# Feed-forward block size by backlog, order of left-over tiles, and a fourth part in the weight conversion

## The chip, the cores and the metric

The kernel runs on one core of a Trainium2 chip. The metric is the device time of one execution in microseconds (us). The engines named below are PE (TensorE, the matmuls), DVE (VectorE), ACT (ScalarE), POOL (GpSimd) and SP (SyncE, which issues the DMAs). Each has its own queue and works through it in order.

## The reference

Attention in which each query keeps only its 32 largest scores, then a feed-forward layer with a hard-swish gate. Eight batches, eight heads, 576 tokens, head size 64; the feed-forward layer sees 4608 tokens of width 512 and has 2048 hidden units. The two weight matrices come as 64-bit floats.

```python
def _attn_ref(q, k, v):
    scores = scale * np.matmul(q, k.transpose(0, 1, 3, 2))
    kth = np.partition(scores, -top_k, axis=-1)[..., -top_k:-top_k + 1]   # top_k = 32
    scores = np.where(scores >= kth, scores, -1000000000.0)
    scores = scores - np.max(scores, axis=-1, keepdims=True)
    attn = np.exp(scores)
    attn = attn / (np.sum(attn, axis=-1, keepdims=True) + 1e-09)
    return np.matmul(attn, v)

def _moe_ref(x, w_in, w_out):
    h = x @ w_in
    g = h * np.clip(h + 3.0, 0.0, 6.0) / 6.0
    return g @ w_out
```

## The kernel before

**Duos.** The 576 queries of a head are four tiles of 128 (query `t` of the loop takes every fourth row) and 64 left-over rows. A *pair* is two heads; a *duo* (class `Duo`, L184) is one query tile of two pairs, so four heads. A batch has ten duos: eight full ones (two halves times four tiles) and two left-over ones (`rest`), whose 64 rows of two heads are stacked to 128 partitions, so they have half as much DVE work. In all there are 80 duos; the list `duos` (L401 to L411) fixes their order. Before the change a left-over duo stands after tile 0 and after tile 2, so at places 2 and 7 of a batch; in the last batch both stand at places 2 and 3.

**Parts of a duo.** `scores` (L199): PE multiplies queries and keys into the PSUM tile `big`, ACT copies them to `sc`. `top` (L242): DVE finds the 32 largest in four rounds of MAX8 (L249) and three of MATCH_REPLACE8 (L253). `shift` (L258, POOL), `exp` (L267, ACT: L272 and L277, and the sum `den`, L282), `inverse` (L284, DVE: the reciprocal, L286), `weights` (L288, POOL: two multiplications at L296 and a copy to `e16` that splits words into 16-bit halves, L305), `flip` (L308: a DMA transpose, issued by SP), `join` (L313: a copy back to `eT`, L317, on ACT for the first half of a duo, u=0, and on POOL for the second, u=1), and `values` (L325: 40 matmul records `pv`, L337, and an ACT copy to `xT` or `xr`, L344).

**Order.** Nothing is scheduled automatically: each engine executes in the order in which the program's main loop (L548 to L578) emits. The loop runs over duos `m`, and within each over eight slots `i`. A slot emits one top round of duo `m` (slots 0 to 3 for u=0, 4 to 7 for u=1), one step of weight conversion, in slot 1 the scores of duo `m+1`, and then the parts that fall due (`parts`, L541). The tables at L524 to L535 say in which slot, counted from a duo's first, each part falls due: `usual` has the reciprocal of u=0 in slot 7 and `values` in slot 20, so in slot 4 of duo `m+2`. There, `values` of duo `m-2` is emitted right ahead of `exp` of duo `m`. Slot 5 also transposes the keys and queries of a pair of the next batch in four duos of each batch.

**Feed-forward.** Once `values` has filled a block of tokens, `queue` (L437) puts a generator `feed_forward` (L348) on `todo`. It is worked off in *pieces* (L420): a piece is eight matmuls of `h` (L361) for 128 tokens, or four for 256, or two of `acc` (L383). A block of 128 tokens has 16 pieces, one of 256 has 32. After each two h pieces come ACT's relu and copy (L369, L371) and POOL's gate (L375, L376), and at the end ACT's scaling to `o` (L393) and the store. `left` counts the pieces queued and not yet emitted. By it each duo takes 6, 7, 8 or 9 pieces (3, 4, 4 or 5 in a left-over duo), spread over its slots:

```python
        level = (left >= 8) + (left >= 16) + (left >= 48)
        count = ((3, 4, 4, 5) if u and u.rest else (6, 7, 8, 9))[level]
```

Blocks have 128 tokens in the first and last batch and 256 in the others (`two`, L465). Left-over rows of two batches make a block of 128 in `xr`. The pool for `xT` has two buffers; so before `values` takes a new one (L467 to L470), it emits all pieces that the block before the last one still has, however many:

```python
            while len(blocks) > 1 and blocks[-2] in todo:
                piece()
```

These are called forced pieces below.

**Weights.** `convert` (L96) turns a chunk of 128 x 512 64-bit floats into 32-bit ones with integer operations. There are 32 chunks, one for each slot from the start. Its parts: the load; then ACT's L108 and L111 and POOL's L109; then DVE's L117 and L118 and POOL's add, L122, which needs L118. `convert_step` (L490) runs one part of the oldest chunk and the first part of a new one.

Of the kernel before, what the change touches and what calls it, by code (L numbers as in the profile page):

```python
# [29 lines left out]
def kernel(  # L30
# [9 lines left out]
    nc = tc.nc  # L40
    P = nc.NUM_PARTITIONS
    B, H, S, D = q.shape
    DM, FF = moe_w_in.shape
    J = S // P
# [51 lines left out]
    def convert(dst, src):  # L96

        st = kqpool.tile([P, 2 * WC], U32, tag="kq", name="st")
        nc.sync.dma_start(st[:], src)
        yield
        words = st[:].rearrange("p (n two) -> p n two", two=2)
        lo, hi = words[:, :, 0], words[:, :, 1]
        a = gpool.tile([P, WC], F32, tag="g", name="a")
        y = gpool.tile([P, WC], F32, tag="g", name="y")
        nc.scalar.activation(a[:], hi.bitcast(F32), AF.Abs)  # L108
        nc.gpsimd.tensor_scalar(a[:], a[:], HI_MOST, HI_LEAST, ALU.min, ALU.max)  # L109

        nc.scalar.activation(y[:], lo, AF.Copy, bias=2.0, scale=2.0**-51)  # L111
        yield

        au, yu = a[:].bitcast(U32), y[:].bitcast(U32)
        nc.vector.tensor_scalar(au, au, 3, None, ALU.logical_shift_left)  # L117
        nc.vector.scalar_tensor_tensor(  # L118
            out=yu, in0=hi, scalar=0x80000000, in1=yu,
            op0=ALU.bitwise_and, op1=ALU.bitwise_or,  # L120
        )
        nc.gpsimd.tensor_tensor(  # L122
            dst.bitcast(I32), a[:].bitcast(I32), y[:].bitcast(I32), ALU.add
        )
# [13 lines left out]
    class Pair:  # L138


        def __init__(self, b, hp):
            self.b, self.hp = b, hp
            self.vm, self.vr, self.kr = vms[hp], vrs[hp], krs[b % 2 * NHP + hp]
# [40 lines left out]
    class Duo:  # L184
# [4 lines left out]


        def __init__(self, pairs, qt):
            self.pairs, self.qt = pairs, qt
            self.rest = qt == J
            self.nt = 1 if self.rest else 2
            self.nb = J + 2 if self.rest else 2 * J + 1
            self.m, self.less = [None] * 2, [None] * 2
            self.e16, self.t16, self.eT = [None] * 2, [None] * 2, [None] * 2
# [115 lines left out]
        def join(self, u):  # L313

            eT = self.eT[u] = kqpool.tile([P, 2 * J + 1, P], F32, tag="kq", name="eT")
            copy = nc.gpsimd.tensor_copy if u else nc.scalar.copy
            copy(  # L317
                eT[:, 0 : self.nb, :]
                .rearrange("p c q -> p (c q)")
                .bitcast(U16)  # L320
                .rearrange("p (x h) -> p h x", h=2),
                self.t16[u][:, 0 : 2 * self.nb, :].rearrange("p (h c) q -> p h (c q)", h=2),
            )
# [77 lines left out]
    pairs = [[Pair(b, hp) for hp in range(NHP)] for b in range(B)]  # L401
    duos = []
    for b in range(B):
        halves = [pairs[b][0:2], pairs[b][2:4]]
        for qt in range(J):
            duos += [Duo(h, qt) for h in halves]

            if b == B - 1 and qt == 0:
                duos += [Duo(h, J) for h in halves]
            elif b < B - 1 and qt % 2 == 0:  # L410
                duos.append(Duo(halves[qt // 2], J))  # L411
    assert J == NHP == 4
    per_batch = 2 * J + 2
    ND = len(duos)
    todo = []
    blocks = []
    left = 0
    gates = []

    def piece(count=1):  # L420
        nonlocal left
        for _ in range(count):
            while todo:
                try:
                    gates.append(next(todo[0]))
                    left -= 1
                    break
                except StopIteration:
                    todo.pop(0)
            else:  # L430
                gates.append(None)
            if len(gates) > 2:
                gate = gates.pop(0)
                if gate:
                    gate()

    def queue(*block):  # L437
        nonlocal left
        todo.append(feed_forward(*block))
        if block[0] is not state.get("xr"):  # L440
            blocks.append(todo[-1])
        left += block[1] // 8

    state = {}

    def values(m):

        u = duos[m]
        b, qt, hp = u.pairs[0].b, u.qt, u.pairs[0].hp
        if u.rest:  # L450
            if b % 2 == 0 and hp == 0:
                state["xr"] = xrpool.tile([P, NHP, P], F32, tag="xr", name="xr")
            u.values(state["xr"][:, hp : hp + 2, (b % 2) * R : (b % 2 + 1) * R])
            if b % 2 == 1 and hp == 2:

                def rows(t0):
                    return [
                        (i * R, (i + 1) * R, out[(b - 1 + i) * S + JP : (b + i) * S, :])
                        for i in range(2)
                    ]  # L460

                queue(state["xr"], P, rows)
            return

        two = 0 < b < B - 1  # L465
        c0 = qt % 2 * P if two else 0
        if hp == 0 and c0 == 0:  # L467
            while len(blocks) > 1 and blocks[-2] in todo:
                piece()
            state["xT"] = xtpool.tile([P, NHP, 2 * P], F32, tag="xT", name="xT")  # L470
        u.values(state["xT"][:, hp : hp + 2, c0 : c0 + P])
        if hp == 2 and (not two or c0):

            def rows(t0):
                t = qt - c0 // P + t0 // P
                return [(0, P, out[b * S + t : b * S + JP : J, :])]

            queue(state["xT"], c0 + P, rows)

    chunks = list(weight_chunks())  # L480
    landing, converting = [], []

    def land(count=1):

        for _ in range(min(count, len(chunks))):
            c = convert(*chunks.pop(0))
            next(c)
            landing.append(c)

    def convert_step(depth=2):  # L490

        if len(converting) >= depth or not landing:
            for c in converting[:1]:
                next(c, None)
            del converting[:1]
        if landing:
            c = landing.pop(0)
            next(c)
            converting.append(c)
        land()  # L500

    def pair_at(m, first):
# [22 lines left out]
        shift0=3, exp0=4, inverse0=7, weights0=8, flip0=10, join0=13,  # L525
        shift1=7, exp1=8, inverse1=11, weights1=12, flip1=14, join1=17, values=20,
    )
    early = dict(
        shift0=3, exp0=3, inverse0=4, weights0=4, flip0=6, join0=8,
        shift1=7, exp1=7, inverse1=8, weights1=8, flip1=10, join1=12, values=13,  # L530
    )
    soon = dict(
        shift0=3, exp0=3, inverse0=5, weights0=5, flip0=7, join0=10,
        shift1=7, exp1=7, inverse1=9, weights1=9, flip1=11, join1=14, values=16,
    )  # L535
    queued = {}
    for m in range(ND):
        for part, at in (early if m < 2 else soon if m >= ND - 2 else usual).items():
            queued.setdefault(8 * m + at, []).append((m, part))

    def parts(slot):  # L541
        for m, part in sorted(queued.get(slot, []), key=lambda x: x[1][:-1] != "shift"):
            if part == "values":
                values(m)
            else:
                getattr(duos[m], part[:-1])(int(part[-1]))

    for m in range(ND + 3):  # L548
        u = duos[m] if m < ND else None

        level = (left >= 8) + (left >= 16) + (left >= 48)
        count = ((3, 4, 4, 5) if u and u.rest else (6, 7, 8, 9))[level]
        for i in range(8):
            if u:
                u.top(i // 4, i % 4)
            convert_step()
            if m == 0 and i == 0:
                first[3].load()
            if m == 0 and i in (1, 2):
                first[i + 1].transpose()  # L560
            if i == (3 if m == 0 else 1) and m + 1 < ND:
                duos[m + 1].scores()
            parts(8 * m + i)
            if m == 0 and i in (1, 4):
                for p in duos[i // 4].pairs:
                    p.load_values()
            if i == 0:
                p = pair_at(m, 4)
                if p:
                    p.load()  # L570
            if i == 3 and u and u.pairs[0].b and 1 <= m % per_batch <= 2:
                for p in duos[m - 1].pairs:
                    p.load_values()
            if i == 5:
                p = pair_at(m, 5)
                if p:
                    p.transpose()
            piece((i + 1) * count // 8 - i * count // 8)  # L578
# [36 lines left out]
```

## Time and profile before

| what | value |
|---|---|
| median of 4 executions | 1632.12 us |
| lowest and highest | 1631.29 and 1633.61 us |
| the profiled execution | 1633.61 us |
| its span on the core | 1631.8 us |
| ACT busy / POOL busy | 1088.5 / 1143.5 us |
| granted PE clock, mean | 0.962 |

The span runs from the first to the last instruction; 1.8 us of the execution's time lie around it. Busy times are sums of an engine's instructions. Lines of the profile have the form: line of the kernel, engine, operation, output, inputs, count. In a timeline a line begins with the start in us from the span's start and the duration; in brackets at its end stands how long the engine was idle ahead of it, and which instruction ended that idle time. A table by stage begins each line with the stretch and its length, then gives busy time and, in brackets, the number of instructions of PE, PEld (weight loads), DVE, ACT and POOL, then the granted clock (1.00 is full), the share of time in which the DMA engines were busy, and GB/s. A line of the waits names the waiting engine and line, the one waited for, and the total, the count and the longest. Below, "duo 27" is the duo with `m` = 27, and PE's lag is how far its queue is behind DVE's.

### The profile page before, as it was taken

To read this page: it belongs to the slowest core of one execution; us is meant where nothing else is said; L and a number is where in the kernel's file an instruction comes from. 1 tells how busy PE (TensorE), PEld (TensorE's weight loads), DVE (VectorE), ACT (ScalarE), POOL (GpSimd) and SP (SyncE) were. 2 spreads that over 40 slices of the span, in tenths; PEclk is the share of its full clock that TensorE was granted. 3 is DMA by queue.
4 is the path that set the end of the run, shared out by engine and by line. 5 is a ranking of instruction groups with operands and counts; after the bars stand their busy time and mean duration, and the time that the engine had idled before them with its cause. 6 is when DMAs were issued, how large, how long until landed. Compare 5 with 4: busy or idle time off the path is not lost.

```text
span 1631.8 us, 25648 instructions
## 1 busy us (share of the span) xinstructions
PE 1471.1 (90%) x8736; PEld 982.6 (60%) x8736; DVE 1470.2 (90%) x3105; ACT 1088.5 (67%) x1863; POOL 1143.5 (70%) x1266
## 2 busy tenths in 40 slices
PE   5237699849999999898999999898999999899999
PEld 3134567527567584756567584656567584657775
DVE  5999999999999989999999889999999889999500
ACT  5566677757777676767767676767767676757521
POOL 3887577757687775867777776867787776867741
PEclk9968799979999999999999999999999999999999
DMA  8553434444444435454344424454344425333310
GB/s 238 149 171 65 102 63 91 94 96 81 75 98 96 94 57 97 85 103 85 65 104 89 94 56 91 88 108 84 65 104 89 94 56 94 80 60 72 65 22 13
DMA packets 450307, 144.29 MB, mean 88 GB/s; under 512 B 433280, under 2 KB 441472, under 8 KB 450176
## 3 DMA queue, kind: packets, MB, share of 16 engines
q1 hardware_dynamic: 450176, 142.65, 42.3%
q8 instruction: 69, 1.13, 0.3%
q14 instruction: 62, 0.51, 0.1%
HBM read 45.09 MB, written 9.44 MB: 33 GB/s over the span
## 4 chain that ended last, share of the span: by engine, by line
DVE 48%; PE 43%; ACT 3%; POOL 3%; issue 1%; SPq 1%; DMA 0%; POOLq 0%; ACTq 0%
DVE m L249 25%; DVE wk L253 20%; PE acc L383 16%; PE h L361 15%; PE pv L337 5%; PE big L226 3%; DVE y L118 1%; POOL eT L317 1%; PE big L229 1%; ACT sc L277 1%; DVE a L117 1%; PE big L176 1%; POOL sc L296 1%; PE big L214 1%; ACT eT L317 0%
## 5 line engine op out<-in xcount | busy, mean ns | idle before, releaser
L249 DVE MAX8 m<-wk 128x8 f32<-128x576 f32 x864 | 614.9, 749 | 3.1
L383 PE MATMUL acc<-w_out,g 128*128 128x512 f32 x1152 | 518.6, 600 | 4.7 <-POOL g L376 4.7
L361 PE MATMUL h<-xT,w_in 128*128 128x256 f32 (+1 forms) x2560 | 471.4, 342 | 0.0
L361 PEld LDWEIGHTS h<-xT,w_in 128*128 128x128 f32 x2560 | 409.1, 194 | 48.1 <-issue 10.3
L253 DVE MATCH_REPLACE8 wk<-m,wk 128x576 f32<-128x576 f32 x576 | 424.1, 743 | 0.0
L383 PEld LDWEIGHTS acc<-w_out,g 128*128 128x128 f32 x1152 | 213.5, 191 | 244.7 <-issue 235.9
L305 POOL COPY e<-sc 128x2304 uint16<-128x2304 uint16 (+1 forms) x192 | 322.4, 1689 | 10.2
L337 PE MATMUL pv<-eT,vm 128*64 128x128 f32 (+1 forms) x2560 | 172.6, 282 | 117.1 <-POOL eT L317 81.3
L272 ACT ACTIVATE sc<-sc,m 128x576 f32<-128x576 f32 x288 | 209.7, 773 | 50.6 <-DVE m L249 50.4
L337 PEld LDWEIGHTS pv<-eT,vm 128*64 128x64 f32 x2560 | 141.2, 146 | 159.9 <-POOL eT L317 86.3
L277 ACT ACTIVATE sc<-sc,shift 128x576 f32<-128x576 f32 x288 | 219.8, 766 | 21.7 <-POOL shift L265 19.0
L296 POOL TENSOR_SCALAR sc<-sc,den 128x576 f32<-128x576 f32 x288 | 213.9, 753 | 27.6 <-DVE den L286 27.0
L262 POOL TENSOR_TENSOR shift<-m 128x2 f32<-128x2 f32 (+1 forms) x160 | 32.2, 201 | 267.3 <-DVE den L286 264.6
L317 POOL COPY eT<-t 128x2304 uint16<-128x2304 uint16 (+1 forms) x80 | 208.8, 2610 | 6.0 <-DMA t<-e 5.8
L253 DVE MATCH_REPLACE8 wk<-m,sc 128x576 f32<-128x576 f32 x288 | 212.0, 743 | 0.0
L317 ACT COPY eT<-t 128x2304 uint16<-128x2304 uint16 (+1 forms) x80 | 208.8, 2610 | 0.0
L249 DVE MAX8 m<-sc 128x8 f32<-128x576 f32 x288 | 203.1, 743 | 1.1 <-ACT sc L235 1.1
L376 POOL TENSOR_TENSOR g<-g,hs 128x512 f32<-128x512 f32 x144 | 184.0, 1278 | 12.0
L344 ACT COPY xT<-pv 128x256 f32<-128x256 f32 x64 | 23.8, 372 | 233.5 <-PE pv L337 233.5
L375 POOL TENSOR_SCALAR g<-g 128x512 f32<-128x512 f32 x144 | 88.8, 617 | 96.4 <-ACT g L369 86.4
L226 PE MATMUL big<-kq 64*128 64x512 f32 x512 | 131.9, 634 | 10.9 <-ACT kr L182 10.8
L369 ACT ACTIVATE g<-h,three 128x512 f32<-128x512 f32 x144 | 98.6, 685 | 62.3 <-PE h L361 61.8
(47 smaller groups left out, 1215.7 us busy)
## 6 DMA issues: line engine op xcount, KB each, us to landing
landed<-in_k_dram SPq DMA_DIRECT2D x64, 128.0 KB, 3.0
landed<-in_q_dram SPq DMA_DIRECT2D x64, 128.0 KB, 2.9
st<-in_moe_w_in_dram SPq DMA_DIRECT2D x16, 512.0 KB, 4.9
vm<-in_v_dram SPq DMA_DIRECT2D x64, 128.0 KB, 2.4
st<-in_moe_w_out_dram SPq DMA_DIRECT2D x16, 512.0 KB, 3.8
out_dram<-o SPq DMA_DIRECT2D x32, 256.0 KB, 2.4
t<-e SPq DMA_TRANSPOSE x160, 4.6
landed<-in_k_dram SPq DMA_DIRECT2D x32, 32.0 KB, 2.6
```

The source lines that it names most:

```text
L226: nc.tensor.matmul(banks[:, 2 * i + hh, :], pr.qT[d, qs], pr.kT[d, :])
L249: nc.vector.max(self.m[u][:, t, 8 * r : 8 * r + 8], self.cur[t])
L253: nc.vector.match_replace(wk, self.m[u][:, t, 8 * r : 8 * r + 8], self.cur[t], LOWEST)
L272: nc.scalar.activation(row, row, AF.Prelu, bias=m[:, t, TOP_K - 1 : TOP_K], scale=-1.0, alpha=FLAT)
L277: nc.scalar.activation(row, row, AF.Exp, bias=self.less[u][:, t : t + 1], scale=-scale / FLAT, accum_out=self.den[:, u, t : t + 1],)
L296: nc.gpsimd.tensor_scalar(row, row, self.den[:, u, t : t + 1], 1.0, ALU.mult, ALU.mult)
L305: nc.gpsimd.tensor_copy(halves[:, :, to : to + c1 - c0], words)
L317: copy(eT[:, 0 : self.nb, :] .rearrange("p c q -> p (c q)") .bitcast(U16) .rearrange("p (x h) -> p h x", h=2), self.t16[u][:, 0 : 2 * self ...
L337: nc.tensor.matmul(pv[hh * D : (hh + 1) * D, u * w : (u + 1) * w], pr.vm[:, hh, c, :] if c < J else pr.vr[:, hh, :], rhs, start=(c == 0), ...
L361: nc.tensor.matmul(h[:, (f - f0) * nt : (f - f0 + 1) * nt], w_in[:, i, f * P : (f + 1) * P], xT[:, i, 0:nt], start=(i == 0), stop=(i == NH ...
L376: nc.gpsimd.tensor_tensor(g[:], g[:], hs[:], ALU.mult)
L383: nc.tensor.matmul(acc[:], gs[f // nf][:, c0 : c0 + P], w_out[:, f, :], start=(f == 0), stop=(f == NFC - 1),)
```

## The change

- Left-over duos of batches 0, 1 and 2 stand last in their batch, both together; batches 3 to 6 and 7 keep their order.
- A block has 256 tokens only if the tile is an even one, the batch isn't the last, and `left` is at least 24 (batches 0 to 2) or 4 (later) when the first half is filled; otherwise it is queued with 128.
- A new `xr` buffer is taken only after the last left-over block is done.
- The conversion's POOL add is a fourth part, run at the start of the next slot's step (`adding`).
- In the first four duos the parts that fall due are emitted ahead of the conversion step, except `inverse` and `weights`, which stay behind it; duo 1's scores move from slot 3 to slot 4.
- In the first two duos `flip` and `values` fall due one slot earlier, and `join` of u=1 is on ACT.

```diff
@@ convert @@
             op0=ALU.bitwise_and, op1=ALU.bitwise_or,
         )
+        yield
         nc.gpsimd.tensor_tensor(
@@ Duo @@
-            self.pairs, self.qt = pairs, qt
+            self.pairs, self.qt, self.early = pairs, qt, False
...
-            copy = nc.gpsimd.tensor_copy if u else nc.scalar.copy
+            copy = nc.gpsimd.tensor_copy if u and not self.early else nc.scalar.copy
@@ the list of duos @@
-            if b == B - 1 and qt == 0:
+            if qt == (0 if b == B - 1 else J - 1) and not 2 < b < B - 1:
                 duos += [Duo(h, J) for h in halves]
-            elif b < B - 1 and qt % 2 == 0:
+            elif 2 < b < B - 1 and qt % 2 == 0:
                 duos.append(Duo(halves[qt // 2], J))
...
+    for u in duos[:2]:
+        u.early = True
@@ values @@
             if b % 2 == 0 and hp == 0:
+                while state.get("rest") in todo:
+                    piece()
...
                 queue(state["xr"], P, rows)
+                state["rest"] = todo[-1]
             return
-        two = 0 < b < B - 1
-        c0 = qt % 2 * P if two else 0
-        if hp == 0 and c0 == 0:
+        if hp == 0 and not state.get("half"):
             while len(blocks) > 1 and blocks[-2] in todo:
                 piece()
             state["xT"] = xtpool.tile([P, NHP, 2 * P], F32, tag="xT", name="xT")
+        c0 = P if state.get("half") else 0
         u.values(state["xT"][:, hp : hp + 2, c0 : c0 + P])
-        if hp == 2 and (not two or c0):
+        if hp == 0:
+            return
+        state["half"] = not c0 and b < B - 1 and qt % 2 == 0 and left >= (24 if b < 3 else 4)
+        if not state["half"]:
@@ convert_step @@
-    def convert_step(depth=2):
-        if len(converting) >= depth or not landing:
+    def convert_step():
+        for c in adding:
+            next(c, None)
+        adding.clear()
+        if len(converting) >= 2 or not landing:
             for c in converting[:1]:
-                next(c, None)
+                next(c)
+            adding.extend(converting[:1])
             del converting[:1]
@@ due slots of the first two duos @@
-        shift0=3, exp0=3, inverse0=4, weights0=4, flip0=6, join0=8,
-        shift1=7, exp1=7, inverse1=8, weights1=8, flip1=10, join1=12, values=13,
+        shift0=3, exp0=3, inverse0=4, weights0=4, flip0=5, join0=8,
+        shift1=7, exp1=7, inverse1=8, weights1=8, flip1=9, join1=12, values=12,
@@ parts and the main loop @@
-    def parts(slot):
+    def parts(slot, late=None):
         for m, part in sorted(queued.get(slot, []), key=lambda x: x[1][:-1] != "shift"):
+            if late is not None and (part[:-1] in ("inverse", "weights")) != late:
+                continue
...
+            if m < 4:
+                parts(8 * m + i, False)
             convert_step()
...
-            if i == (3 if m == 0 else 1) and m + 1 < ND:
+            if i == (4 if m == 0 else 1) and m + 1 < ND:
                 duos[m + 1].scores()
-            parts(8 * m + i)
+            if m < 4:
+                parts(8 * m + i, True)
+            else:
+                parts(8 * m + i)
```

More of the change, by code (lines that the diff above doesn't have):

```diff
@@ L480 @@
     chunks = list(weight_chunks())
-    landing, converting = [], []
+    landing, converting, adding = [], [], []
     def land(count=1):
```

## The prediction

> **What bounds the kernel now.** I read the DVE's waits first, then a busy table by stage, then the timeline around each large wait. DVE (top-32 rounds) and PE are both busy 1470 us of 1632, so neither total decides: the question is where each stands still.
>
> ```profile
> PE 1471.1 (90%) x8736; PEld 982.6 (60%) x8736; DVE 1470.2 (90%) x3105; ACT 1088.5 (67%) x1863; POOL 1143.5 (70%) x1266
> ```
> ```profile
> DVE den L286 <- ACT den L282: 49.6, 20, 10.0
> DVE a L117 <- POOL a L109: 10.6, 2, 10.4
> ```
> ```profile
> 60.00:120.00 60.00, 20.69 (x142) 16.04 (x139) 57.16 (x93) 34.32 (x60) 49.98 (x50) 0.77 0.58 170
> 120.00:420.00 300.00, 244.29 (x1613) 171.32 (x1612) 298.60 (x634) 211.02 (x363) 215.60 (x239) 0.89 0.43 83
> 420.00:1440.00 1020.00, 994.19 (x5738) 652.85 (x5737) 984.09 (x2108) 725.92 (x1243) 745.11 (x829) 0.99 0.43 86
> ```
> Columns of the last: PE, PEld, DVE, ACT, POOL busy, clock. Between 120 and 420 us PE idles 56 us while DVE is full; between 420 and 1440 PE is nearly full and DVE loses 36 us. Nearly all of DVE's idle time is in front of its reciprocal (L286), at few places:
>
> ```profile
> 40.34 0.17 DVE L286 RECIPROCAL den<-den 128x2 f32<-128x2 f32 x1 [7.61 <-ACT den L282]
> 576.03 0.16 DVE L286 RECIPROCAL den<-den 128x1 f32<-128x1 f32 x1 [5.96 <-ACT den L282]
> 944.21 0.16 DVE L286 RECIPROCAL den<-den 128x1 f32<-128x1 f32 x1 [9.99 <-ACT den L282]
> 1310.94 0.16 DVE L286 RECIPROCAL den<-den 128x1 f32<-128x1 f32 x1 [9.92 <-ACT den L282]
> 1414.13 0.16 DVE L286 RECIPROCAL den<-den 128x1 f32<-128x1 f32 x1 [1.90 <-ACT den L282]
> 1475.09 0.17 DVE L286 RECIPROCAL den<-den 128x2 f32<-128x2 f32 x1 [2.65 <-ACT den L282]
> 1538.47 0.17 DVE L286 RECIPROCAL den<-den 128x2 f32<-128x2 f32 x1 [4.73 <-ACT den L282]
> ```
> The ACT timeline tells why at 576:
>
> ```profile
> 569.69 0.60 ACT L393 ACTIVATE o<-acc 128x512 f32<-128x512 f32 x1 [6.36 <-PE acc L383]
> 573.76 0.37 ACT L344 COPY xT<-pv 128x256 f32<-128x256 f32 x1 [3.47 <-PE pv L337]
> ```
> `values` (L468) found the block before the last still queued and forced five pieces of feed-forward onto PE ahead of the pv matmuls. ACT waits for them, the exponentials stand behind ACT's copies, and DVE waits for den. By the loop's counters (`left`, `count`) duo 27 forces 5 pieces, duos 47 and 67 force 7 each, duo 76 five: these are the stalls at 576, 944, 1311 and 1475. DVE's last work ends at 1538.6; PE then works off 93.2 us more. So the time is DVE's work, plus its stalls, plus this tail.
>
> **The skill.** "TensorE: Matmul & The Clock Gate", Architectural detail, calls ACT and DVE strict FIFO queues: the two ACT lines agree, the exponentials had their operands and still stood behind o and xT. The same page's Part 1 has PE at half clock after idling; the trace shows 0.77 granted in 60 to 120 us. "SBUF — State Buffer", Who interferes with whom, says that a DVE instruction with two SBUF inputs waits for a GpSimd instruction that reads SBUF, and that whoever issues first holds the port. The trace agrees: L118 took 2.58 us at 58.91 beside POOL's e copy, 0.68 where POOL was idle.
>
> **Prices.** A 128-token block takes 14.29 us (h) and 13.75 (acc) at the end of the chain, 16 pieces, so 1.75 us a piece. In 256-token blocks the h part runs 40 matmuls in 8.83 us, 28.3 us for 128, so 14.1 per 128 tokens: the block size hardly matters to PE (five pairs of 128 in place of five 256 add about 1.7 us in all). Scores 1.92 + 0.64 = 2.56 us, of a left-over duo (38.3 + 9.8) / 16 = 3.0; values 2.35; one pair's transposes 1.5. DVE: from 944.21 to 1310.94 lie 16 full and 4 left-over duos, 366.7 us less 10.6 of stalls, so 19.8 us for a full duo and 9.9 for a left-over one. A full duo with 8 pieces costs PE 14.0 + 2.56 + 2.35 = 18.9, just under DVE; a left-over duo with 4 pieces costs 11.9 to 13.4, over DVE's 9.9.
>
> **1. Start (m < 4).** Now exp0 of duo 0 stands on ACT behind the conversion of a chunk (1.3 us) and the copies of scores(1), which wait 3.76 us for PE and take 2.2. Changed, it follows the kr copies at 30.07: Prelu 1.45, exponentials and reads 1.62, den 0.2, ready at 33.4. DVE reaches the reciprocal at 32.7, so 7.61 becomes about 0.7: -6.9. Scores(1) comes one slot later; DVE needs it four slots on (over 10 us), so it is free. Shift no longer stands behind L122, which waits for DVE: the waits of ACT for shift (2.96, 2.97, 3.78 us) go, and with them DVE's 0.62, 0.63 and 2.00: -3.2. Join of u=1 of two duos moves from POOL to ACT (2.8 us each, ACT is half idle there), flip and values come one slot earlier: DVE waits for none of these; at nothing. On SP the flip now stands ahead of the slot's chunk load and waits there for POOL's weights, so loads behind it (chunks, keys, values) go out up to 5 us later (two passes 1.5, copy 2.1 to 3.0). A chunk lies ready about two slots of 3.9 us before ACT takes it and lands in 4.9 us, which hides most; ACT waited for chunks 2.0 us in all. Without that cover each of the four early flips could cost DVE a few us; bounds 0 and +5, I take 0. Start: -10.1.
>
> **2. The add in a fourth part.** 32 adds of 1.28 us stay on POOL, one slot later, behind shift and weights instead of ahead; a DVE pair L117/L118 no longer holds POOL up (0.63 to 1.6 us each, 14 us in all). POOL has the room. Each chunk's a and y live a slot longer in the eight g buffers; ACT's wait for them is 10.4 us now and does not reach DVE. Contention at the port: L117 and L118 take 56.7 us against 32 x 1.09 = 35 at their fastest, so 22 us hang on what POOL does beside them. No row shows the new order; bounds are -10 (half of it goes) and +6 (some adds now meet L118). I take 0, since the same POOL work still follows each L118.
>
> **3. Left-over duos in pairs at the end of batches 0 to 2.** A pair exists now, duos 72 and 73: DVE lost 0.49 and 1.90, because the eT of the duo before comes late when slots are half as long. Singles lose 0.3 to 0.95. For pairs 8/9 and 18/19: together +3.3. The third is in step 4.
>
> **4. Block size by backlog.** By the counters the changed kernel has `left` 25 where it had 25 at duo 20, but has queued 16 pieces more by then, and 20 more pieces are done by duo 30; those are 35 us of the 56 that PE idled. From duo 33 to 41 it uses up that lead (left 6 instead of 19), so at 47 nothing is forced (-10.0), at 67 five instead of seven, with the same counters as duo 27 now, so 6.0 instead of 9.9 (-3.9). From duo 68 on counters and order are the same as now, so the tail of 93.2 us stays.
> The price is at the end of batch 2, where `left` stays over 16 and each duo takes 8. What slack PE has: in duo 27 now, between two pv's, 11 pieces 19.3 + 1.5 + 2.56 + 2.35 = 25.7 against DVE's 13.6; 12.1 over, 5.96 lost, so about 6 us of slack; duo 47 gives 15.6 less 9.99, the same; duo 76, 7.9 less 2.65, 5.2. Changed, duo 26: 14 pieces (6 forced) 24.5 + 6.4 = 30.9 against 19.8, 11.1 over; less the slack, and with a bit more of it in a full duo, 5 lost. Duo 28, a left-over one: 9 pieces (3 forced) 15.8 + 1.5 + 3.0 + 2.35 = 22.6 against 13.6, and the slack is spent: 9. Duo 29: 13.4 against 9.9: 3.5. Sum 17.5 against 6.0 now: +11.5.
>
> **Sum.** -10.1 + 3.3 + 11.5 - 10.0 - 3.9 = -9.2. The profiled execution took 1633.6 (span 1631.8), 1.5 over the median of 1632.1; the same difference puts the median at 1623.
>
> **Rivals.**
> A, the start's gain is lost again: once the wait for den goes, L117 waits for a, or L118 for POOL. For it: POOL runs at 50 of 60 us in 60 to 120. Against: L117 waited for POOL only twice. The 10.1 goes: 1633.
> B, the pile-up in batch 2 costs little: a full duo may hold more slack than I took, and the pieces come at full clock. Then 17.5 falls to about 7: 1612.
> C, slower: PE becomes the bound in duos 16 to 26, where it now has eight pieces a duo. That needs a low clock: 120 to 420 us ran at 0.89 on the average. Ten duos at 18.9 to 20.4 us are 190 us of PE work at full clock; at 0.9 they are 211, less 6 of slack: 15 us of new stalls, 1638. It decides from a granted clock under about 0.92 in 320 to 520 us. Against: the idle gaps are why the clock is low, and these are filled.
>
> **Numbers.** Forecast 0.50 (1616 to 1629), A 0.13, B 0.20, C 0.17. About 0.2% (3.3 us) is what a measurement can tell from no change. Faster: 0.48 + 0.20 = 0.68; same 0.14, nearly all of A; slower 0.18. The range reaches from B with some port gain to C: 1609 to 1638.
>
> **What would show it.** Start: DVE's wait of 7.61 at L286 under 1.5, duo 1 begun some 7 us sooner. Step 4: no stall of 10 us near 935; one near 6 at the place of 1311; and two or three stalls of 3 to 9 us in a row between 550 and 620. Tail: DVE's last line some 93 us before the end. I am wrong if the stalls of batch 2 sum to over 25 us, if DVE stalls at each duo around 400 to 520 (C), or if L117 and L118 move by more than 6 us in all.

## The result and the profile after

The changed kernel takes 1628.49 us (median of 34 runs) against 1631.43 of the kernel before in the same series: ratio 0.9982, 95% interval 0.9977 to 0.9987. That is 2.9 us less. I had forecast 9 us less (1623). The way and the range were right, the size was not, and three things that I had priced at nothing (join and values ahead of the conversion step, the fourth part, the work of L117 and L118) each turned out to be worth several us.

The waits of DVE in the changed kernel (waiting engine and line, releaser, total, times, longest):

```profile
DVE den L287 <- ACT den L283: 43.8, 20, 7.1
DVE a L117 <- POOL a L109: 16.7, 5, 10.3
DVE m L250 <- ACT sc L236: 1.7, 1, 1.7
```
The waits for den fell from 49.6 to 43.8 us, but those of L117 for POOL rose from 10.6 to 16.7. With the small ones the sum is 63.0 us against 62.1: DVE stands still as long as before, only elsewhere. The busy times say where the gain came from:

```profile
PE 1471.5 (90%) x9376; PEld 1001.4 (62%) x9376; DVE 1465.6 (90%) x3105; ACT 1095.6 (67%) x1865; POOL 1143.4 (70%) x1264
```
DVE is busy 4.6 us less (L117 and L118 together took 51.1 us, 56.7 before). DVE's last instruction starts at 1534.92 instead of 1538.47, and 93 us of PE follow in both, so the span is 3.6 us shorter.

DVE's main waits one by one, in the timeline of the changed kernel (start, duration, in brackets the idle time ahead):

```profile
33.23 0.17 DVE L287 RECIPROCAL den<-den 128x2 f32<-128x2 f32 x1 [0.66 <-ACT den L283]
...
78.84 1.48 DVE L117 TENSOR_SCALAR a<-a 128x512 uint32<-128x512 uint32 x1 [4.06 <-POOL a L109]
...
166.88 0.17 DVE L287 RECIPROCAL den<-den 128x2 f32<-128x2 f32 x1 [3.28 <-ACT den L283]
...
572.92 0.17 DVE L287 RECIPROCAL den<-den 128x2 f32<-128x2 f32 x1 [5.24 <-ACT den L283]
...
611.69 0.16 DVE L287 RECIPROCAL den<-den 128x1 f32<-128x1 f32 x1 [7.12 <-ACT den L283]
...
1307.04 0.16 DVE L287 RECIPROCAL den<-den 128x1 f32<-128x1 f32 x1 [6.51 <-ACT den L283]
```
The 7.61 at the start is 0.66, the stall of 9.99 near 944 is gone, that near 1311 is 6.51, and the end of batch 2 costs a row of stalls: 5.24, 0.68, 7.12, 1.27 and 2.05. So far as forecast. New and not forecast are the second and third line.

By stage (PE, PEld, DVE, ACT, POOL busy; clock; DMA share; GB/s), changed kernel:

```profile
60.00:120.00 60.00, 28.26 (x206) 23.35 (x207) 55.94 (x105) 41.43 (x66) 42.54 (x45) 0.66 0.54 173
120.00:420.00 300.00, 256.52 (x1756) 175.65 (x1754) 290.22 (x618) 207.19 (x353) 223.16 (x240) 0.94 0.44 85
420.00:1440.00 1020.00, 976.54 (x6190) 660.03 (x6192) 985.29 (x2109) 725.79 (x1243) 743.83 (x831) 0.98 0.43 86
```
PE is busy 12 us longer between 120 and 420 us (244.3 before), as the new block rule wants. DVE, which was full there (298.6 of 300), now loses 10 us.

What made L117 wait at 78.84 is on ACT and POOL. The two timelines:

```profile
65.46 2.77 ACT L318 COPY eT<-t 128x2304 uint16<-128x2304 uint16 x1
70.75 0.37 ACT L345 COPY xT<-pv 128x256 f32<-128x256 f32 x1 [2.53 <-PE pv L338]
71.02 0.67 ACT L108 ACTIVATE a<-st 128x512 f32<-128x512 f32 x1
```
```profile
71.78 0.61 POOL L109 TENSOR_SCALAR a<-a 128x512 f32<-128x512 f32 x1 [4.17 <-ACT a L108]
72.49 2.23 POOL L297 TENSOR_SCALAR sc<-sc,den 128x576 f32<-128x576 f32 x2
74.78 2.10 POOL L306 COPY e<-sc 128x2304 uint16<-128x2304 uint16 x1
76.84 1.26 POOL L123 TENSOR_TENSOR w_in<-a,y 128x512 int32<-128x512 int32 x1
78.19 0.61 POOL L109 TENSOR_SCALAR a<-a 128x512 f32<-128x512 f32 x1
```
In the first four duos join and values now stand ahead of the slot's conversion step. ACT copies eT for 2.8 us, then waits for the pv matmuls, and the chunk's L108 stands behind both. POOL waits for it 4.17 us with the weights behind it; when they have run, the next chunk's L109 comes at 78.19, and DVE has waited 4.06 us for it. I read this from the trace alone; the experiments had to say whether it was the reason, and whether the new fourth part had a share.

### The profile page after: what moved, and what is told of

The parts are those of the page before. It is cut to its first block, busy times and chain, and to the rows that moved or that the text cites. A ratio compares the mean times of both kernels' runs of the same rounds, so it can differ in the third digit from the quotient of the medians.

```text
span 1628.2 us, 26916 instructions
## 1 busy us (share of the span) xinstructions
PE 1471.5 (90%) x9376; PEld 1001.4 (62%) x9376; DVE 1465.6 (90%) x3105; ACT 1095.6 (67%) x1865; POOL 1143.4 (70%) x1264
## 4 chain that ended last, share of the span: by engine, by line
DVE 54%; PE 32%; POOL 7%; ACT 4%; issue 2%; SPq 1%; DMA 0%; POOLq 0%; ACTq 0%
DVE m L250 29%; DVE wk L254 24%; PE acc L384 12%; PE h L362 12%; PE pv L338 4%; PE big L227 2%; POOL e L306 1%; POOL sc L297 1%; POOL eT L318 1%; POOL w_out L123 1%; ACT sc L278 1%; ACT eT L318 1%; PE big L230 1%; POOL a L109 1%; ACT sc L273 1%
## 5 line engine op out<-in xcount | busy, mean ns | idle before, releaser
L362 PE MATMUL h<-xT,w_in 128*128 128x128 f32 (+1 forms) x3200 | 476.0, 308 | 0.0
L362 PEld LDWEIGHTS h<-xT,w_in 128*128 128x128 f32 x3200 | 434.8, 193 | 34.0 <-issue 10.8
L338 PE MATMUL pv<-eT,vm 128*64 128x128 f32 (+1 forms) x2560 | 169.1, 278 | 100.7 <-POOL eT L318 54.0
L263 POOL TENSOR_TENSOR shift<-m 128x2 f32<-128x2 f32 (+1 forms) x160 | 33.5, 209 | 275.7 <-DVE den L287 273.4
L338 PEld LDWEIGHTS pv<-eT,vm 128*64 128x64 f32 x2560 | 137.5, 143 | 145.0 <-POOL eT L318 59.6
L318 ACT COPY eT<-t 128x2304 uint16<-128x2304 uint16 (+1 forms) x82 | 214.5, 2616 | 1.7 <-DMA t<-e 1.7
L318 POOL COPY eT<-t 128x2304 uint16<-128x2304 uint16 (+1 forms) x78 | 203.0, 2602 | 5.9 <-DMA t<-e 4.4
L370 ACT ACTIVATE g<-h,three 128x512 f32<-128x512 f32 x144 | 98.9, 687 | 68.5 <-PE h L362 66.1
```

The source lines that it names most:

```text
L318: copy(eT[:, 0 : self.nb, :] .rearrange("p c q -> p (c q)") .bitcast(U16) .rearrange("p (x h) -> p h x", h=2), self.t16[u][:, 0 : 2 * self ...
L338: nc.tensor.matmul(pv[hh * D : (hh + 1) * D, u * w : (u + 1) * w], pr.vm[:, hh, c, :] if c < J else pr.vr[:, hh, :], rhs, start=(c == 0), ...
L362: nc.tensor.matmul(h[:, (f - f0) * nt : (f - f0 + 1) * nt], w_in[:, i, f * P : (f + 1) * P], xT[:, i, 0:nt], start=(i == 0), stop=(i == NH ...
```

## The experiments

Theory 1: the start's gain is real, and ACT, held by join and the copy to xT, gives it back. Theory 3 (there is no theory 2): the fourth part costs time because it holds the buffers of the pool g longer. The rivals: the fourth part's place on POOL makes L117 wait; or the conversion's rate is the limit and the wait only moves; or the loss sits in the blocks and in the order of left-over duos. All ratios are to the kernel before, measured in the same series as the run; in brackets stands the 95% interval.

**The parts of the change alone.** Three kernels, each the kernel before with one group of edits.

e1_start_only: all edits of the first four duos, as in the diff above: parts ahead of the step, table, joins on ACT, scores in slot 4.

> The kernel before with only the start's edits: parts ahead of the conversion step in the first four duos, scores of duo 1 in slot 4, flips and values of the first two duos a slot earlier, their joins of u=1 on ACT. No fourth part, old blocks, old order of left-over duos. Theory 1 (the start gains 10 us at the reciprocal, and ACT, held by the copy to xT that waits for PE, gives part of it back as waits of DVE's L117 for POOL's L109): the wait of 7.61 goes to about 0.7, some 4 us of L117 waits appear, ratio 0.996 to 0.998. Rival (the L117 waits come from the fourth part, whose add stands behind weights on POOL): no L117 waits here, ratio about 0.994.

Measured 0.9981 (0.9975 to 0.9988), 3.2 us less: as much as the whole change gains. DVE's two largest waits:

```profile
DVE den L286 <- ACT den L282: 36.7, 13, 10.0
DVE a L117 <- POOL a L109: 21.6, 5, 10.4
```
The reciprocal lost 12.9 us of waits, L117 got 11.0 new ones (4.05, 4.71 and 2.16 after 75 us), and there is no fourth part in this kernel. The rival that put these waits on the fourth part falls. They are more than the 4 us that theory 1 expected. In the trace a join does it without the copy, too: ahead of the wait of 4.71 there is no copy to xT on ACT, only a join from 84.84 to 87.59; the chunk's L108 follows it, POOL's L109 waits 1.90 us for that, the weights follow, and the next L109 comes at 94.61.

e2_add_only:

```diff
             op0=ALU.bitwise_and, op1=ALU.bitwise_or,
         )
+        yield
         nc.gpsimd.tensor_tensor(
```
(and `adding` in `convert_step`).

> The kernel before with only the POOL add as a fourth part. Theory 1: no new wait of DVE, L117 and L118 shrink by 0 to 4 us in sum, ratio 0.998 to 1.000. Rival (the fourth part makes L117 wait): L117 waits of 4 to 6 us after 60 us, ratio 1.002 to 1.004.

Measured 1.0007 (0.9999 to 1.0015). No new wait of L117, as theory 1 has it, so the rival falls; but theory 1's range (0.998 to 1.000) missed as well: L117 and L118 took 59.6 us, 2.9 more than before, where they were to take less.

e3_blocks_order: only the block rule and the places of left-over duos.

> The kernel before with only the block size by backlog and the left-over duos last in batches 0 to 2. By the changed kernel's stalls (pairs of left-over duos +5, batch 2 +10, the stall near 944 -10, near 1311 -3.5) these two parts together are worth about +1 us: ratio 0.999 to 1.002. The rival, that the prediction's loss sits in these parts and the start did gain 10: ratio 1.003 to 1.005.

Measured 0.9994 (0.9986 to 1.0002). The stalls in batch 2 and at duo 67 are those of the changed kernel (5.23, 7.13, 2.04 in batch 2, 6.50 near 1309). So these two parts are worth nothing that can be told; the rival falls. The three medians differ from before by -3.2, +1.2 and -0.7 us, together -2.7, against -2.9 for the whole change. The sum agrees, but the waits are not the same ones: two of the three new waits of e1 are not in the changed kernel, and its 3.28 at the reciprocal near 167 is in none of the three.

**What the start loses to.** e5_values13:

```diff
-        shift1=7, exp1=7, inverse1=8, weights1=8, flip1=9, join1=12, values=12,
+        shift1=7, exp1=7, inverse1=8, weights1=8, flip1=9, join1=12, values=13,
```


> The changed kernel with values of the first two duos back in slot 13, all else as changed. Theory 1 (ACT's copy to xT waits for PE ahead of a chunk's ACT part, so L109 comes after weights on POOL, so L117 waits 4.06 us near 79): the wait goes to under 1.5, ratio to before 0.995 to 0.997. Rival (POOL is full there, or the eight g buffers hold ACT): the wait stays at 3 to 5 us and the ratio at 0.998.

Measured 0.9993 (0.9985 to 1.0001). The wait near 79 is gone, as theory 1 said, so there the copy to xT made it. But theory 1's range (0.995 to 0.997) missed, and the time is no better: the wait of L117 near 142, 0.86 in the changed kernel, is now 3.98. A second obstacle stood behind the first.

e9_exp_first leaves only shift and exp ahead of the step:

```diff
-            if late is not None and (part[:-1] in ("inverse", "weights")) != late:
+            if late is not None and (part[:-1] not in ("shift", "exp")) != late:
```


> The changed kernel, but in the first four duos only shift and exp stand ahead of the conversion step; flip, join and values stay behind it. Theory 1 (join and the copy to xT, which wait for a DMA and for PE, hold the chunk's ACT part up): the L117 wait of 4.06 near 79 goes to under 1.5; the waits near 142 and 167 that the fourth part makes stay; ratio 0.996 to 0.998. Rival (the conversion's own rate is the limit, so the wait only moves): waits of L117 still sum to 5 or more, ratio 0.998 to 0.9995.

Measured 0.9977 (0.9968 to 0.9987). The wait near 79 is gone (0.53) and the time is in theory 1's range, but can't be told from the changed kernel's: L117's waits after the first still sum to 7.0 us, as the rival had it, 3.98 of them at 141, and the reciprocal's 3.23 stands at 166. So the wait does move, and what it moves to was still to be found.

e6_no_add is the changed kernel with the `yield` and the use of `adding` taken out.

> The changed kernel without the fourth part (the add follows L118 in the same step again). Theory 3 (the fourth part holds a and y a slot longer in the eight g buffers, which the first feed-forward block needs too; ACT then waits for L123, and the waits near 142 and 167 follow): those two (0.9 and 3.3 us) go, the L117 waits after 75 us stay, ratio 0.9970 to 0.9978. Rival (the fourth part pays, by unblocking POOL): ratio 0.9985 or more.

Measured 0.9970 (0.9958 to 0.9982), as theory 3 had it. The waits near 142 and 167 are gone, the 4.05 near 79 stays. So the fourth part makes the two later waits, and the reorder the first one.

e10_exp_first_alone: the kernel before with e9's edit and scores in slot 4, old table, no fourth part, old blocks.

> The kernel before with shift and exp ahead of the conversion step in the first four duos and duo 1's scores in slot 4, and nothing else: old table, old joins, no fourth part, old blocks. Theory 1: the reciprocal's waits go (7.61 to 0.7, 3.25 to 0), L117 waits sum to under 2, ratio 0.993 to 0.995. Rival (the conversion's own rate takes back what DVE gains): L117 waits of 8 to 11 us as with all the start's edits, ratio 0.998.

Measured 0.9953 (0.9941 to 0.9965), 7.1 us less; theory 1 had 0.993 to 0.995. DVE's two largest waits:

```profile
DVE den L286 <- ACT den L282: 38.2, 13, 10.0
DVE a L117 <- POOL a L109: 10.7, 2, 10.1
```
L117 is back at its first wait and 0.5 us, the reciprocal keeps the gain. This is the start that I had forecast as a part of the change: 11.4 us of the reciprocal's waits gone, of which the time shows 7 to 9 (span 1622.6 against 1631.8; DVE is busy 1.4 us longer and waits 0.6 longer for the first scores). The rival "the conversion's own rate is the limit" falls.

e16_g10 asks why the fourth part costs. It is e9_exp_first, fourth part included, with

```diff
-    kqpool = pool("kq", 13)
+    kqpool = pool("kq", 12)
-    gpool = pool("g", 8)
+    gpool = pool("g", 10)
```


> The changed kernel with only shift and exp ahead of the conversion step (so the fourth part is in), and ten buffers in the pool g in place of eight, twelve in kq in place of 13 to make room. Theory 3 (the fourth part's cost is that a and y hold the g buffers a slot longer, so ACT waits for L123 once the first feed-forward block takes g buffers too): the waits of DVE near 141 (3.98) and 166 (3.23) fall under 1 each, ratio 0.9945 to 0.996. Rival (the add's late place on POOL is the cost): both stay, ratio 0.997 to 0.9985.

Measured 0.9930 (0.9916 to 0.9944): 1620.9 us, where e9 with eight buffers had 0.9977. The waits at 141 and 166 are gone, so the rival falls; the time is a little under theory 3's range (0.9945 to 0.996). In e9 ACT's waits for the adds between 40 and 150 us were

```profile
ACT a L108 <- POOL w_in L123: 7.0, 3, 3.3
ACT y L111 <- POOL w_out L123: 6.9, 2, 6.2
ACT a L108 <- POOL w_out L123: 6.1, 4, 2.4
...
ACT g L370 <- POOL w_out L123: 3.9, 1, 3.9
```
and with ten buffers two of the four are left:

```profile
ACT a L108 <- POOL w_out L123: 5.4, 3, 2.9
...
ACT g L370 <- POOL w_out L123: 2.9, 1, 2.9
```
L108, L111 and L370 all write tiles of the pool g. The add L123 reads a and y, and until it has run their buffers can't be written. With a slot more per chunk and the first feed-forward block taking g tiles from the same eight, ACT stands at L111 for 6.2 us and at L370 for 3.9, and all behind it with it. From L370 the way to DVE can be followed in e9:

```profile
135.33 0.69 ACT L370 ACTIVATE g<-h,three 128x512 f32<-128x512 f32 x1 [3.93 <-POOL w_out L123]
140.28 0.61 POOL L109 TENSOR_SCALAR a<-a 128x512 f32<-128x512 f32 x1 [4.98 <-ACT a L108]
140.92 0.43 DVE L117 TENSOR_SCALAR a<-a 128x512 uint32<-128x512 uint32 x1 [3.98 <-POOL a L109]
```
Between the first and the second line ACT runs an exp and the chunk's L108, which stand behind L370. That is theory 3, and two runs bear it out by different edits: e6 takes the fourth part away, e16 gives it buffers. Neither the smaller kq pool nor ten g buffers without the fourth part was tried by itself.

**Forced pieces, blocks and order.** e12_exp_first_blocks: e10 with the block rule and the order of the changed kernel.

> The kernel before with shift and exp ahead of the conversion step (as in the run before), and block size by backlog and left-over duos last in batches 0 to 2; no fourth part, old table. Theory 1: the two gains add, ratio 0.993 to 0.995, some 4 us or more under the changed kernel. Rival: at 0.997 to 0.998, no better than the changed kernel.

Measured 0.9958 (0.9946 to 0.9970), the same as e10 within the interval, and below the changed kernel by 3.5 us. Theory 1's range (0.993 to 0.995) missed: there were no two gains to add, since blocks and order had none to give.

e13_blocks_alone: e10 with the block rule, left-over duos in their old places.

> The best start so far (shift and exp ahead of the conversion step, old table, no fourth part) with block size by backlog alone; left-over duos in their old places. The counters force 3 pieces at duo 25, 3 at 27, 5 at 47, 7 at 67, 5 at 76. Theory (forced pieces in a left-over duo make the stalls, and the pairs of left-over duos made the changed kernel pay 16 us in batch 2): stalls near 6 at duo 27, 6 at 47, 10 at 67, together 4 less than with the old blocks; no row of stalls in batch 2; ratio 0.991 to 0.9945. Rival (what block size wins is PE work that only moves, so the sum stays): ratio 0.995 to 0.996, as with the start alone.

Measured 0.9959 (0.9946 to 0.9971). My theory's range (0.991 to 0.9945) missed. No row of stalls in batch 2, as I had said, and 6.52 in place of 9.98 near 936; but duo 27 lost 7.39 (6.49 in e10), and the small waits for den of 0.3 to 1.8 us after 100 us sum to 6.8 instead of 3.8; all of DVE's waits sum to 52.9 us, 51.4 in e10. The rival's range holds: the sum of the stalls stays. That the block rule only moves PE's work to another place is its reading; no run tried it further.

e14_three_xT: e10 with three buffers of xT, so that nothing is forced.

```diff
-    kqpool = pool("kq", 13)
+    kqpool = pool("kq", 12)
-    xtpool = pool("xt", 2)
+    xtpool = pool("xt", 3)
...
-            while len(blocks) > 1 and blocks[-2] in todo:
+            while len(blocks) > 2 and blocks[-3] in todo:
```


> The best start so far with three buffers of xT in place of two (and 12 in place of 13 in the pool kq, to make room), old blocks, old order: no piece is forced any more. Theory (forced pieces make the stalls): the stalls near 569, 936, 1302 and 1466 fall from 6.5, 10, 10 and 2.7 to under 3 each, DVE ends some 25 us earlier; but left is 47 instead of 35 when DVE ends, so the tail grows by 12 pieces, 21 us: ratio 0.991 to 0.995. Rival A (the stalls come from PE's total work, so they return elsewhere): DVE's waits stay at about 50 us in sum, ratio 0.995 or more. Rival B (all 25 us count): ratio 0.980.

Measured 0.9921 (0.9909 to 0.9934), 12.8 us less. DVE's two largest waits, and its last line:

```profile
DVE a L117 <- POOL a L109: 10.9, 2, 10.4
DVE den L286 <- ACT den L282: 8.5, 7, 4.7
```
```profile
1499.52 0.17 DVE L286 RECIPROCAL den<-den 128x2 f32<-128x2 f32 x1 [4.69 <-ACT den L282]
```
The four stalls at the forced pieces are gone with them, so the theory holds and rival A (they come back elsewhere) falls. DVE ends 29.7 us before e10's (1529.19), but the span is only 4.3 us shorter (1618.3 against 1622.6): the tail after DVE grew from 93.2 to 118.6 us, since the pieces that were not forced are done there; so rival B (all of it counts) falls too. This is why a stall of DVE in the middle is worth so little here: PE is nearly full, and what it does not do under a stall it does at the end.

e15_combined joins what held: e10's start, three xT buffers, the block rule, left-over duos last in batch 0 alone, no fourth part, and

```diff
-        level = (left >= 8) + (left >= 16) + (left >= 48)
+        level = (left >= 8) + (left >= 16) + (left >= 24)
```


> The best start so far, three buffers of xT, block size by backlog, left-over duos last in batch 0 only, and nine pieces a duo from a left of 24 instead of 48. The counters force nothing, and left is 31 at duo 80 instead of 35. Theory: stalls of a few us are spread over duos 27 to 70, DVE ends 15 to 25 us before the 1529 of the start alone, the tail is some 7 us shorter than with the old counts: ratio 0.980 to 0.988. Rival (one kq buffer less or PE's lag gives it back): 0.990 or more.

Measured 0.9877 (0.9862 to 0.9892): 1612.6 us, 16 under the changed kernel and 20 under the one before. Two lines of its page of waits and its last reciprocal:

```profile
DVE den L286 <- ACT den L282: 30.7, 23, 4.7
DVE a L117 <- POOL a L109: 11.5, 3, 10.5
```
```profile
1522.12 0.17 DVE L286 RECIPROCAL den<-den 128x2 f32<-128x2 f32 x1 [4.74 <-ACT den L282]
```
DVE waits more than in e14, 31 us for den instead of 9, in small portions, and ends 22.6 us later; the tail is 89.6 us instead of 118.6. The sum decides, not DVE's waits. The ratio is in the theory's range, but its two terms missed: DVE was to end 15 to 25 us before e10's 1529 and ends 7 before it, and the tail was to be some 7 us shorter than with the old counts (93.2) and is 3.6 shorter. Which of the joined edits does what was not taken apart.

## Why the prediction was right and wrong

**The chain of reasons held.** The time is DVE's work, its stalls and a tail: the tail is 93 us in both kernels, and the span fell by as much as DVE's end, 3.6 us.

**Step 4 was right in size, step 3 nearly.** Batch 2 was to cost 17.5 us and cost 16.4; the stall at duo 47 was to go and went; that at duo 67 was to be 6.0 and is 6.5. Pairs 8/9 and 18/19 were to cost 3.3 and cost 5.7 (0.78 and 2.05, 1.05 and 1.77), mostly since I took too much off for the single ones. Forecast for these steps together +0.9 (+3.3 + 11.5 - 10.0 - 3.9); the run with these edits alone is 0.7 us faster, with an interval that reaches from -2.3 to +0.3. The small waits I left out account for part of it.

**Step 1 failed in one sentence.** The prediction said of join, flip and values, moved ahead of the conversion step: "DVE waits for none of these; at nothing." DVE doesn't wait for them itself, but ACT works in order, and the chunk's L108 now stands behind a join and behind a copy that waits for PE; POOL's L109 and DVE's L117 follow. The gain at the reciprocal was as forecast (7.61 to 0.66, the 3.2 us of small ones gone), and instead of nothing 11.0 us of it came back at L117 in the run with the start's edits alone, 6.1 in the changed kernel. Leaving these parts behind the step, with the table and joins as they were, made the start's gain 7.1 us instead of 3.2; how much of that is the order and how much the table and the joins was not taken apart. So the gain was lost two queues away from the engine that I watched, to a delay that I had not followed through.

**Step 2 had the right place and the wrong bound.** I saw that a and y live a slot longer in the eight g buffers, and wrote that ACT's wait for them "does not reach DVE". Alone, in e2, it didn't. Together with the earlier start it does: 0.86 and 3.28 us in the changed kernel, 3.98 and 3.23 with e9's order. Ten buffers removed both, and the ratio went from 0.9977 to 0.9930. With both faults out, the changed kernel gains 11.7 us. That this is near the 9 I had forecast is in part luck: e12, which has neither fault, has only 0.9958, though DVE waits no longer in it (52.9 us in sum, 55.1 in e16); what differs on DVE is L117 and L118, 51.9 us in e16 and 56.7 in e12.

**The rivals.** A (the start's gain is lost at L117) was the true case for the start, with the right engine and line waited for; I gave it 0.13, because L117 waited for POOL only twice before. But that count came from a kernel in which none of these parts stood ahead of L108. It gave 1633 as it had nothing for the 4 to 5 us that DVE's busy time fell by. B did not happen: batch 2 cost 16.4 us, not 7. C did not either: no stall at each duo around 400 to 520, and the granted clock in 320 to 520 us was 0.99. Its 15 us were also too many by its own prices: 211 us of PE work belong against the 198 that ten full duos take on DVE, not against PE's own 190, which leaves 7.

**Contention.** I took 0 within -10 and +6. L117 and L118 together took 51.1 us in the changed kernel, 56.7 before, and between 49.4 (e9) and 59.6 (e2) in the runs. The saving of 5.6 us is about as large as what the kernel gained. By the waits alone, 0.9 us longer than before, the changed kernel would not have been faster at all, so as far as these two profiles go, that the forecast had the way right is luck. Whether the saving belongs to the change is left open: each figure is one profiled execution. The kernels with low sums are mostly those in which DVE waited longer for POOL just ahead of L117, but e3 (53.6) and e16 (51.9) are not among these. The rule of the Trainium skill that the prediction used ("SBUF — State Buffer", Who interferes with whom) would fit: most of the saving is L118's, which has two inputs (33.5 us before, 28.9 after), and what DVE has waited ahead of the pair it may not have to wait in it. No run shows that this is the reason.

## What to carry to other kernels

Before a step is moved ahead of another on an in-order queue, list how long the moved step takes and what it waits for itself (here 2.8 us for a join, and for the copy PE's matmuls), and follow who stands behind it through every queue: ACT, POOL, DVE. A tile that lives one step longer takes a buffer from every other user of its pool: count them all, at the time at which they meet (the fourth part alone made no wait of DVE, with the earlier start it made two). And where two engines are both nearly full, a stall that is taken off one of them is worth only what the other one's remaining work at the end allows: price the tail with it.

## What the runs showed of the hardware

The mean granted PE clock between 60 and 120 us went down, from 0.77 to 0.66, although PE was busy longer there (28.3 us in place of 20.7); e10 and e14 show the same (0.65 and 0.64, 27.4 and 27.8 us busy). Between 120 and 420 us, where gaps were filled, it rose from 0.89 to 0.94. The Trainium skill ("TensorE: Matmul & The Clock Gate", Part 1) ties the clock to how busy PE has been; the second pair of numbers agrees with that, the first goes the other way. The clock was not tried by itself, so why it fell there is open.
